# An attention and feed-forward kernel: first x block and v rows in order of use on one DMA queue, small loads behind them, and another order of the weight folds

## The chip, the cores and the metric

One core of one Trainium2 chip runs one program. The metric is the time of that program on the device, in microseconds, and lower is better. TensorE is called PE here, VectorE DVE, ScalarE ACT, GpSimd POOL and SyncE SP, as in the profile.

## The reference, cut to what matters

```python
# B=1, S=2048, D=640, H=32 heads of Dh=20, F=1728; bf16
g = sigmoid((x * gate_w).sum(-1, keepdims=True))
q, k, v = heads(x @ wqkv)                       # [H, S, Dh] each
phi(u)  = concat([softmax(u @ w_phi[h]), softmax(-(u @ w_phi[h]))])
kv, z   = phi(k).T @ v, phi(k).sum(over S)      # linear attention, not causal
a       = (phi(q) @ kv) / (phi(q) @ z + 1e-6) @ wo
b       = (gelu(x @ w_gate) * (x @ w_up)) @ w_down
out     = g * a + (1 - g) * b
```

`q @ w_phi` is linear in x, so the kernel multiplies `w_phi` into the key and query weights first. It calls this a fold: five folds for the keys and five for the queries, one for each 128 rows of the weights. The gate weights become one more column of the keys' weights.

## The kernel before

Only the first 30 us matter here. The x of the first four tiles of 128 tokens is loaded as it lies and transposed on PE. The x of the later tiles and the weights to be folded come by transposing DMA loads (`dma_start_transpose`, called turned loads below). All loads of the SP queue are issued in the order of the program. `sc.op` and `sc.dma` add the semaphore waits that the named reads and writes call for, so each engine's order is the order of the program.

```python
        x4 = self.x[0:self.BT, :].rearrange("(p j) n -> p j n", j=self.TB)

        def xload(q, j):                  # two rows of each group of four: 320 KB
            sc.dma(q, lambda e: e.dma_start(self.xtok[:, j:j + 2, :], x4[:, j:j + 2, :]), ...)
# ... (wload: one turned load of 640 x 640 weights; xturn(t, n): turned x of tiles t to t+n-1)
        sc.op("pool", lambda e: e.memset(self.gz[:, :], 0.0), writes=["gz"])
        xload("sp", 0)
        xload("act", 2)
        sc.dma("act", lambda e: e.dma_start(
            self.wphi_sb[:, :, :], self.wphi.rearrange("h d f -> (h d) f").rearrange("(i p) f -> p i f", p=P)),
            writes=["wphi"])
        for kt in range(KD):
            sc.dma("sp", lambda e: e.dma_start(self.w3[:, kt, 0:D], w3[:, kt, 2 * D:3 * D]), writes=[("wv", kt)])
        sc.dma("act", lambda e: e.dma_start(self.gz[0:KD, :], self.gw.rearrange("(k p) -> k p", p=P)), writes=["gz"])
        xturn(4, 2)
        wload(self.wkT, D, "wkT")
        xturn(6, 2)
        wload(self.wqT, 0, "wqT")
        xturn(8, 4)
        xturn(12, 4)
# ... (then the feed-forward weights)
```

The start of PE's program, and the order of the folds (`f`), of v (`v_early`), of the keys (`k_early`) and of the query projections (`pq`):

```python
        warm(7)                           # 7 matmuls of 512 columns on a zeroed tile
        xt(0, 6, "d"); xt(1, 7, "a"); xt(2, 2, "d"); xt(3, 3, "a")   # PE transposes, DVE or ACT copies
        # ... v of tiles 0-3, step by step over the five v rows: 4 x 2 matmuls for each row
        # ... before the last row: self.blockdiag() (w_phi), self.gate_column(6) (gate row, a PE transpose)
        self.v_early(4, 6)
        self.v_early(5, 0)
        f(0, "k", (2, 3), "d")
        f(1, "k", (4, 5), "a")
        self.v_early(6, 6)
        f(2, "k", (2, 3), "d")
        f(3, "k", (4, 5), "a")
        f(4, "k", (0, 1), "d")
        self.v_early(7, 6)
        self.k_early(0, 2)
        f(0, "q", (4, 5), "d")
        f(1, "q", (6, 7), "d")
        self.k_early(1, 0)
        f(2, "q", (4, 5), "d")
        f(3, "q", (6, 7), "d")
        self.k_early(2, 2)
        f(4, "q", (4, 5), "d")
        self.k_norm(0)
        self.k_early(3, 0)
        self.k_norm(1)
        self.pq(0, 1, 1)
        self.pq(0, 0, 0)
        self.pq(0, 3, 3)
        self.columns = True
        self.gram(0)
```

PE writes its results into numbered banks, and `pq` takes bank 6 or 7 in turn, so the third one waits until ACT has read the first one's bank:

```python
    def pq(self, b, i, n):
        sc = self.sc
        bank = 6 + n % 2
        # ... five matmuls, then two ACT exponentials out of that bank
```

`gram(t)` (PE's product of phi(k) and v for tile t) needs `k_norm(t)`: a sum, a reciprocal and two products on DVE, 1.48 + 0.55 + 1.56 us by the timeline.

The softmax here doesn't subtract the row's maximum and nothing guards it: scores larger than these inputs give would overflow.

Of the kernel before, what the change touches and what calls it, by code (L numbers as in the profile page):

```python
# [3 lines left out]
P = 128  # L4
BF16 = mybir.dt.bfloat16
F32 = mybir.dt.float32
AF = mybir.ActivationFunctionType
# [100 lines left out]
class _Kernel:  # L108
    S, D, H, DH, F = 2048, 640, 32, 20, 1728
    KD = D // P  # L110
# [31 lines left out]
    def alloc(self):  # L142
        nc = self.nc
        S, D, KD, NT, BT, NFC, DH = self.S, self.D, self.KD, self.NT, self.BT, self.NFC, self.DH
        T = nc.alloc_sbuf_tensor
        self.xT = T("xT", [P, KD, S], BF16)
        self.wo_sb = T("wo_sb", [P, KD, D], BF16)
        self.wg_sb = T("wg_sb", [P, KD, 13 * P], BF16)
        self.wu_sb = T("wu_sb", [P, KD, 13 * P], BF16)
        self.wgu_sb = T("wgu_sb", [P, KD, P], BF16)  # L150
        self.wd_sb = T("wd_sb", [P, NFC, D], BF16)
        self.Eq = T("Eq", [P, 2, KD, S], BF16)
        self.KV = T("KV", [P, KD, 2, self.HB * self.DB], BF16)
        self.hmask = T("hmask", [P, 2, KD, self.HB], BF16)
        self.mask = T("mask", [P, KD, 8], BF16)
        self.ident = T("ident", [P, P], BF16)
        self.zero = T("zero", [P, 512], BF16)
        self.gz = T("gz", [P, P], BF16)
        self.gcol = T("gcol", [P, NT], F32)
        self.gtmp = T("gtmp", [P, NT], F32)  # L160
        self.Gm = T("Gm", [P, NT], F32)
        self.Gr = T("Gr", [P, NT], F32)
        self.BD = T("BD", [P, KD, 8 * DH], BF16)
        self.wphi_sb = T("wphi_sb", [P, KD, DH], BF16)

        def place(lists):
            size = {"b": 0}
            plans = []
            for items in lists:
                c = 0  # L170
                for name, shape, dt in items:
                    n = mybir.dt.size(dt)
                    for s_ in shape[1:]:
                        n *= s_
                    c = (c + 31) // 32 * 32
                    plans.append((name, shape, dt, c))
                    c += n
                size["b"] = max(size["b"], c)
            arena = T("arena%d" % len(self._arenas), [P, size["b"]], mybir.dt.uint8)
            self._arenas.append(arena)  # L180
            base = nc.lookup_mloc(arena).addr
            for name, shape, dt, c in plans:
                setattr(self, name, nc.alloc_sbuf_tensor_at(name, shape, dt, offset=base + c))
        self._arenas = []
        place([
            [("w3", [P, KD, 2 * D + 2], BF16), ("wq2", [P, KD, D], BF16)],
            [("hT0", [P, NFC, BT], BF16), ("gl", [P, 3, BT], BF16)],
        ])
        place([
            [("Ek", [P, self.NSE, 2, D], BF16), ("vaug", [P, self.NSV, self.H, self.DA], BF16),  # L190
             ("Dk", [P, self.NSE, 2, 2 * self.H], F32)],
            [("hT1", [P, NFC, BT], BF16)],
        ])
        place([
            [("xtok", [P, self.TB, D], BF16), ("wkT", [P, KD, D], BF16), ("wqT", [P, KD, D], BF16)],
            [("goT", [P, 8, KD, P], BF16), ("O1", [P, 2, D], BF16), ("O2", [P, 2, D], BF16),
             ("Og", [P, 2, D], BF16), ("RH", [P, 2, 8, 2, 16], F32), ("outsb", [P, 4, D], BF16)],
        ])
        self.ps = nc.alloc_psum_tensor("ps", [P, 4096], F32)
# [8 lines left out]
    def loads(self):  # L208
        sc, nc = self.sc, self.nc
        D, KD, DH, P_ = self.D, self.KD, self.DH, P  # L210
        w3 = self.wqkv.rearrange("(kt p) n -> p kt n", p=P)

        x4 = self.x[0:self.BT, :].rearrange("(p j) n -> p j n", j=self.TB)

        def xload(q, j):
            sc.dma(q, lambda e: e.dma_start(self.xtok[:, j:j + 2, :], x4[:, j:j + 2, :]),
                   writes=[("xtok", j), ("xtok", j + 1)])

        def wload(T, c0, key):
            sc.dma("sp", lambda e: e.dma_start_transpose(T[:, :, :], self.wqkv[:, c0:c0 + D]), writes=[key])  # L220

        def xturn(t, n):
            a, z = t * P, (t + n) * P
            sc.dma("sp", lambda e: e.dma_start_transpose(self.xT[:, :, a:z], self.x[a:z, :]),
                   writes=[("xT", k) for k in range(t, t + n)])
        sc.op("pool", lambda e: e.memset(self.gz[:, :], 0.0), writes=["gz"])
        xload("sp", 0)
        xload("act", 2)
        sc.dma("act", lambda e: e.dma_start(
            self.wphi_sb[:, :, :], self.wphi.rearrange("h d f -> (h d) f").rearrange("(i p) f -> p i f", p=P)),  # L230
            writes=["wphi"])
        for kt in range(KD):
            sc.dma("sp", lambda e: e.dma_start(self.w3[:, kt, 0:D], w3[:, kt, 2 * D:3 * D]), writes=[("wv", kt)])
        sc.dma("act", lambda e: e.dma_start(self.gz[0:KD, :], self.gw.rearrange("(k p) -> k p", p=P)), writes=["gz"])
        xturn(4, 2)
        wload(self.wkT, D, "wkT")
        xturn(6, 2)
        wload(self.wqT, 0, "wqT")
        xturn(8, 4)
        xturn(12, 4)  # L240
        half = 7 * P
# [10 lines left out]
        for r in (0, 1):  # L252
            sc.dma("sp", lambda e: e.dma_start(self.wd_sb[64 * r:64 * r + 64, 13, :], self.wd[13 * P:self.F, :]),
                   writes=[("wd13", r)])
        sc.dma("sp", lambda e: e.dma_start(self.wo_sb[:, :, :], self.wo.rearrange("(kt p) n -> p kt n", p=P)),
               writes=["wo"])
# [61 lines left out]
    def fold(self, kt, which, banks, ekey):  # L318
        sc = self.sc
        DH = self.DH  # L320
        wT = self.wkT if which == "k" else self.wqT
        for i in range(self.KD):
            lo, hi = self.HLO[i], self.HHI[i]
            for h in (0, 1):
                a, z = max(lo, 16 * h), min(hi, 16 * h + 15)
                if a > z:
                    continue
                n = (z - a + 1) * DH
                b, c0, k0 = banks[h], (a - 16 * h) * DH, (a - lo) * DH
                first, fin = (i == 0 or a == 16), (z in (15, 31) and i in (2, 4))  # L330
                sc.op("pe", lambda e: e.matmul(  # L331
                    self.bank(b)[:, c0:c0 + n], wT[:, i, kt * P:(kt + 1) * P], self.BD[:, i, k0:k0 + n],
                    start=first, stop=fin, skip_group_check=True),
                    reads=["w%sT" % which, ("BD", i)], writes=[("ps", b)], signal=fin)
        src = self.pair(banks)
        if which == "k":
            dst = self.w3[:, kt, self.D:2 * self.D].rearrange("p (b c) -> p b c", c=320)
        else:
            dst = self.wq2[:, kt, :].rearrange("p (i r c) -> p r i c", r=2, c=64)
            src = src.rearrange("p r (i c) -> p r i c", c=64)  # L340
        rd = [("ps", b) for b in banks]
        wr = [("w%s2" % which, kt)]
        if ekey == "d":
            self.sc.op("dve", lambda e: e.tensor_copy(dst, src), reads=rd, writes=wr)
        else:
            self.sc.op("act", lambda e: e.activation(dst, src, AF.Copy), reads=rd, writes=wr)
# [161 lines left out]
                      writes=[("KV", i, r, g)])  # L508
                self.kvk[i, r].append(("KV", i, r, g))

    def pq(self, b, i, n):
        sc = self.sc
        bank = 6 + n % 2
        for kt in range(self.KD):
            self.mm(bank, 0, 512, self.wq2[:, kt, i * P:(i + 1) * P], self.xT[:, kt, b * self.BT:(b + 1) * self.BT],
                    kt == 0, kt == self.KD - 1, [("xT", t) for t in range(4 * b, 4 * b + 4)] + [("wq2", kt)])
# [15 lines left out]
    def attention_state(self):  # L532
        NT = self.NT
        order = [(b, i) for b in range(self.NB) for i in range(self.KD)]
        sc = self.sc
        sc.op("dve", lambda e: e.memset(self.zero[:, :], 0.0), writes=["zero"])

        def warm(n):
            for i in range(n):
                sc.op("pe", lambda e: e.matmul(self.bank(0), self.zero[:, 0:P], self.zero[:, :], start=True, stop=True),  # L540
                      reads=["zero"], writes=[("ps", 0)])
        vs, ve, xt = self.v_step, self.v_first_evac, self.x_transpose
        warm(7)
        xt(0, 6, "d")
        xt(1, 7, "a")
        xt(2, 2, "d")
        xt(3, 3, "a")
        for t in range(4):
            vs(t, 0)
        for t in range(4):  # L550
# [11 lines left out]
                ve([0, 1, 2], "a", True)  # L562
        ve([3], "d", True)
        f = self.fold
        self.v_early(4, 6)
        self.v_early(5, 0)
        f(0, "k", (2, 3), "d")
        f(1, "k", (4, 5), "a")
        self.v_early(6, 6)
        f(2, "k", (2, 3), "d")  # L570
        f(3, "k", (4, 5), "a")
        f(4, "k", (0, 1), "d")
        self.v_early(7, 6)
        self.k_early(0, 2)
        f(0, "q", (4, 5), "d")
        f(1, "q", (6, 7), "d")
        self.k_early(1, 0)
        f(2, "q", (4, 5), "d")
        f(3, "q", (6, 7), "d")
        self.k_early(2, 2)  # L580
        f(4, "q", (4, 5), "d")
        self.k_norm(0)
        self.k_early(3, 0)
        self.k_norm(1)
        self.pq(0, 1, 1)
        self.pq(0, 0, 0)
        self.pq(0, 3, 3)
        self.columns = True
        self.gram(0)
        self.k_norm(2)  # L590
# [2 lines left out]
        n = 4  # L593
# [47 lines left out]
    def num(self, t):  # L641
        sc = self.sc
        NBK = self.NUMB
        DB, DH = self.DB, self.DH
        old = [("xtok", k) for k in range(4)] + ["wkT", "wqT"]
        w = self.HB * DB
        for i in range(self.KD):
            for s in (0, 1):
# [190 lines left out]
```

## Time and profile before

| | before |
|---|---|
| time, median (range) of the 6 runs beside the changed kernel | 288.97 us (288.30 to 289.33) |
| span of the profiled run | 287.9 us |
| PE busy | 282.0 us, 98% |
| first x transposed / first v matmul / v of tile 4 | 4.72 / 6.40 / 12.29 us |
| key folds / query folds / first gram begin | 14.79 / 20.75 / 30.26 us |

The head of the page and the busy time of each engine:

```profile
span 287.9 us, 7001 instructions
...
PE 282.0 (98%) x3017; PEld 185.7 (65%) x3032; DVE 174.8 (61%) x353; ACT 105.0 (36%) x199; POOL 5.3 (2%) x36
...
```

PE has almost no idle time to give back. What is left lies in the first 30 us. The timeline of PE shows it; its columns are start, length, engine, line, operation, output<-inputs, form, count, and in brackets the idle time before and what ended it:

```profile
...
1.25 3.17 PE L540 MATMUL ps<-zero 128*128 128x512 bf16 x7 [1.25 <-DVE zero L536]
4.72 1.83 PE L290 MATMUL ps<-ident,xtok 128*128 128x128 bf16 x20 [0.30 <-DMA xtok<-in_A_x_dram]
6.40 4.69 PE L363 MATMUL ps<-w,xT 128*128 128x480 bf16 x32
...
12.29 2.67 PE L351 MATMUL ps<-w,xT 128*128 128x512 bf16 x19
14.79 0.79 PE L331 MATMUL ps<-BD,wkT 128*128 128x140 bf16 x12
15.45 1.53 PE L351 MATMUL ps<-w,xT 128*128 128x512 bf16 x10
...
20.75 0.80 PE L331 MATMUL ps<-BD,wqT 128*128 128x140 bf16 x12
...
26.63 2.10 PE L351 MATMUL ps<-xT,wq 128*128 128x512 bf16 x9
29.08 1.25 PE L351 MATMUL ps<-xT,wq 128*128 128x512 bf16 x5 [0.34 <-ACT Eq L518]
30.26 0.48 PE L449 MATMUL ps<-Ek,vaug 128*64 128x120 bf16 x11
...
```

The first 4.7 us are warm-up and waiting for x. From there PE runs through to 29.08, where the third query projection waits for ACT. The x19 at 12.29 is one matmul record short (20 were issued), so v of tile 4 really began about 0.2 us earlier. The warm-up matmuls start 0.427 us apart and the first transposes 0.107 us apart; from 5.90 us on the transposes are 0.056 us apart. The Trainium skill (TensorE: Matmul & The Clock Gate, Part 1) gives 106.7 and 426.7 ns for a cold array at 128 and 512 columns and about 56 ns for a warm one at 128, so this trace agrees. The page's row of granted clock shows 9 in every slice and does not tell the two apart.

The waits of PE and of its weight loads (PEld) in the first 32 us: engine, line, what it waited for, total us, times, longest.

```profile
...
PEld ps L290 <- DMA xtok<-in_A_x_dram: 1.2, 1, 1.2
...
PE ps L351 <- ACT Eq L518: 0.3, 1, 0.3
...
PEld ps L331 <- DMA wqT<-in_A_wqkv_dram: 0.3, 1, 0.3
...
```

The loads, by the list of DMA issues (queue, operation, count, KB each, median us from issue to landing):

```profile
...
w<-in_A_wqkv_dram SPq DMA_DIRECT2D x5, 160.0 KB, 4.0
...
xtok<-in_A_x_dram ACTq DMA_DIRECT2D x1, 320.0 KB, 3.6
xtok<-in_A_x_dram SPq DMA_DIRECT2D x1, 320.0 KB, 3.9
...
xT<-in_A_x_dram SPq DMA_TRANSPOSE x4, 5.4
...
wkT<-in_A_wqkv_dram SPq DMA_TRANSPOSE x1, 6.9
wqT<-in_A_wqkv_dram SPq DMA_TRANSPOSE x1, 8.8
...
```

In the trace each of these loads signals 16 times (the gate row 6 times), and the last signal is the landing. The two x pieces land at 4.43 and 4.68 us, the v rows from 5.26 to 7.23, the keys' weights at 13.11, the turned x of tiles 6 and 7 at 15.40, the queries' weights at 20.70. The last two are used at 15.45 and 20.75. So PE follows close behind the turned loads.

### The profile page before, as it was taken

To read this page: it belongs to the slowest core of one execution; us is meant where nothing else is said; L and a number is where in the kernel's file an instruction comes from. 1 tells how busy PE (TensorE), PEld (TensorE's weight loads), DVE (VectorE), ACT (ScalarE), POOL (GpSimd) and SP (SyncE) were. 2 spreads that over 40 slices of the span, in tenths; PEclk is the share of its full clock that TensorE was granted. 3 is DMA by queue.
4 is the path that set the end of the run, shared out by engine and by line. 5 is a ranking of instruction groups with operands and counts; after the bars stand their busy time and mean duration, and the time that the engine had idled before them with its cause. 6 is when DMAs were issued, how large, how long until landed. Compare 5 with 4: busy or idle time off the path is not lost.

```text
span 287.9 us, 7001 instructions
## 1 busy us (share of the span) xinstructions
PE 282.0 (98%) x3017; PEld 185.7 (65%) x3032; DVE 174.8 (61%) x353; ACT 105.0 (36%) x199; POOL 5.3 (2%) x36
## 2 busy tenths in 40 slices
PE   7999999999999999999999999999999999999996
PEld 4566689999994444444577544457754445777785
DVE  2338999999977553568588142258823324883801
ACT  3357897687663322322111332211133231112111
POOL 7000000000000000000000000000000000000000
PEclk9999999999999999999999999999999999999999
DMA  7999996000002000011014200001330000132221
GB/s 232 191 166 240 368 367 204 0 2 2 2 0 48 0 0 0 3 24 23 2 25 86 78 0 0 0 3 25 57 96 11 0 0 2 25 45 78 67 72 48
DMA packets 36937, 18.67 MB, mean 65 GB/s; under 512 B 28970, under 2 KB 36394, under 8 KB 36906
## 3 DMA queue, kind: packets, MB, share of 16 engines
q1 hardware_dynamic: 36096, 17.86, 24.8%
q8 instruction: 24, 0.39, 0.6%
q10 hardware_dynamic: 810, 0.35, 0.5%
q14 instruction: 7, 0.06, 0.1%
HBM read 9.04 MB, written 2.62 MB: 40 GB/s over the span
## 4 chain that ended last, share of the span: by engine, by line
PE 96%; DMA 1%; ACT 1%; issue 1%; ACTq 0%
PE ps L351 60%; PE ps L708 28%; PE ps L651 2%; PE ps L363 2%; PE ps L449 2%; DMA xtok<-in_A_x_dram 1%; PE ps L331 1%; PE ps L290 1%; ACT Ek L413 0%; ACT Eq L518 0%; ACT outsb L721 0%; ACT gcol L416 0%; PE ps L313 0%; ACTq L42 0%
## 5 line engine op out<-in xcount | busy, mean ns | idle before, releaser
L625 DVE TENSOR_TENSOR hT<-ps,gl 128x512 bf16<-128x512 f32 x52 | 35.7, 690 | 65.1 <-PE ps L351 65.0
L708 PE MATMUL ps<-wd_sb,hT 64*128 64x320 bf16 (+2 forms) x918 | 66.2, 288 | 0.0
L351 PE MATMUL ps<-xT,wg_sb 128*128 128x512 bf16 (+1 forms) x265 | 63.8, 379 | 0.6 <-issue 0.5
L351 PE MATMUL ps<-xT,wu_sb 128*128 128x512 bf16 (+1 forms) x263 | 63.3, 379 | 0.5 <-issue 0.2
L623 ACT ACTIVATE gl<-ps 128x512 bf16<-128x512 f32 x52 | 30.9, 596 | 70.3 <-PE ps L351 66.0
L708 PEld LDWEIGHTS ps<-wd_sb,hT 64*128 64x128 bf16 x918 | 43.1, 94 | 15.6 <-ACT gl L623 0.8
L351 PEld LDWEIGHTS ps<-xT,wu_sb 128*128 128x128 bf16 (+1 forms) x270 | 26.5, 99 | 29.7 <-DVE hT L625 0.5
L351 PEld LDWEIGHTS ps<-xT,wg_sb 128*128 128x128 bf16 (+1 forms) x270 | 26.0, 99 | 29.1 <-issue 0.5
L721 ACT ACTIVATE outsb<-ps,Gm 128x320 bf16<-128x320 f32 (+2 forms) x31 | 14.5, 515 | 75.6 <-PE ps L708 75.6
L351 PE MATMUL ps<-w,xT 128*64 128x512 bf16 (+6 forms) x398 | 41.6, 325 | 0.2
L351 PEld LDWEIGHTS ps<-w,xT 128*64 128x64 bf16 (+1 forms) x400 | 35.8, 107 | 4.8
L708 PE MATMUL ps<-wo_sb,goT 64*128 64x320 bf16 (+2 forms) x340 | 27.8, 288 | 0.0
L351 PE MATMUL ps<-xT,wq 128*64 128x512 bf16 (+1 forms) x184 | 26.1, 380 | 0.4 <-ACT Eq L518 0.3
L433 DVE TENSOR_TENSOR Ek<-Ek,Dk 128x640 bf16<-128x640 bf16 x32 | 25.0, 822 | 0.6
L678 DVE TENSOR_TENSOR O<-ps,RH 128x640 bf16<-128x640 f32 x32 | 24.7, 814 | 0.0
L424 DVE TENSOR_REDUCE Dk<-Ek 128x64 f32<-128x1280 bf16 x16 | 23.7, 1479 | 0.1
L413 ACT ACTIVATE Ek<-ps 128x640 bf16<-128x640 f32 x32 | 20.7, 703 | 3.7 <-PE ps L351 3.7
L518 ACT ACTIVATE Eq<-ps 128x512 bf16<-128x512 f32 x40 | 21.7, 605 | 1.1 <-PE ps L351 0.8
L708 PEld LDWEIGHTS ps<-wo_sb,goT 64*128 64x128 bf16 x340 | 16.1, 94 | 5.4
L351 PEld LDWEIGHTS ps<-xT,wq 128*64 128x64 bf16 (+1 forms) x185 | 15.3, 108 | 3.4 <-ACT Eq L518 0.8
L405 ACT ACTIVATE vaug<-ps 128x640 bf16<-128x640 f32 x12 | 8.5, 706 | 12.1 <-PE ps L351 12.1
L667 DVE RECIPROCAL RH<-ps 128x32 f32<-128x32 f32 x16 | 5.7, 357 | 7.5 <-PE ps L651 6.8
(65 smaller groups left out, 148.0 us busy)
## 6 DMA issues: line engine op xcount, KB each, us to landing
out_dram<-outsb SPq DMA_DIRECT2D x7, 320.0 KB, 2.3
wd_sb<-in_B_w_down_dram SPq DMA_DIRECT2D x1, 2080.0 KB, 14.2
wg_sb<-in_B_w_gate_dram SPq DMA_DIRECT2D x1, 1120.0 KB, 5.8
wu_sb<-in_B_w_up_dram SPq DMA_DIRECT2D x1, 1120.0 KB, 8.3
wg_sb<-in_B_w_gate_dram SPq DMA_DIRECT2D x1, 960.0 KB, 9.6
wu_sb<-in_B_w_up_dram SPq DMA_DIRECT2D x1, 960.0 KB, 10.2
w<-in_A_wqkv_dram SPq DMA_DIRECT2D x5, 160.0 KB, 4.0
wo_sb<-in_A_wo_dram SPq DMA_DIRECT2D x1, 800.0 KB, 9.9
```

The costliest lines, as they stand in the source:

```text
L351: self.sc.op("pe", lambda e: e.matmul(self.ps[a:z, bank * 512 + c0:bank * 512 + c0 + n], lhs[:, a:z], rhs, start=first, stop=fin), reads=r ...
L363: sc.op("pe", lambda e, c0=c0, n=n, bk=bk, col=col: e.matmul(self.bank(bk)[:, col:col + n], self.xT[:, kt, t * P:(t + 1) * P], self.w3[:, ...
L405: self.sc.op("act", lambda e: e.activation(self.vaug[:, sv, :, 0:self.DH], self.bank(B, self.D).rearrange("p (h d) -> p h d", d=self.DH), ...
L413: self.sc.op("act", lambda e, s=s, scale=scale: e.activation(self.Ek[:, se, s, :], self.ps[:, o:o + self.D], AF.Exp, scale=scale), reads=[ ...
L424: sc.op("dve", lambda e: e.tensor_reduce(self.Dk[:, se, 0, :].rearrange("p (s h) -> p s h", h=H), self.Ek[:, se, :, :].rearrange("p s (h d ...
L433: sc.op("dve", lambda e, v=v, r=r: e.tensor_tensor(v, v, r, ALU.mult), reads=[("Rk", se)], writes=[("Ek", se, s)])
L518: sc.op("act", lambda e, s=s, scale=scale: e.activation(self.Eq[:, s, i, b * self.BT:(b + 1) * self.BT], self.bank(bank), AF.Exp, scale=sc ...
L623: sc.op("act", lambda e: e.activation(self.gl[:, slot, :], self.bank(banks[0]), AF.Gelu_apprx_tanh), reads=[("ps", banks[0])], writes=[("g ...
L625: sc.op("dve", lambda e: e.tensor_tensor(hT[:, c, :], self.bank(banks[1]), self.gl[:, slot, :], ALU.mult), reads=[("ps", banks[1]), ("gl", ...
L678: dve(lambda e, o=o, f=f, s=s: e.tensor_tensor(o, V[s][:, :, :, 0:DH], f, ALU.mult), rb + [key(6 + s)], [("O", s, sl)], guard=old)
L708: sc.op("pe", lambda e: e.matmul(self.bank(bk, w), lhs, rhs, start=opens and x == 0, stop=end and not opens, skip_group_check=True), reads ...
L721: sc.op("act", lambda e: e.activation(dst, self.bank(bk, w), AF.Copy, scale=g), reads=rd, writes=wr)
```

## The change

Its intent is that each transfer comes in the order of its use. The x block comes in four pieces and v in one row and two pairs, all on the SP queue; the two small loads go out later on the ACT queue, behind an ACT copy. The warm-up reads a constant, so that it starts sooner. The key folds stand in a row, the query folds behind the second keys, so that neither waits for its weights. The third query projection gets bank 0.

```diff
         def xload(q, j):
-            ...(self.xtok[:, j:j + 2, :], x4[:, j:j + 2, :])
+            ...(self.xtok[:, j, :], x4[:, j, :])
 # ... (a helper vload; wload split by rows, used for all rows at once)
-        xload("sp", 0)
-        xload("act", 2)
-        sc.dma("act", ... wphi ...)
-        for kt in range(KD):
-            sc.dma("sp", ... v row kt ...)
-        sc.dma("act", ... gate row ...)
+        sc.op("act", ... activation(gtmp, const 1.0, AF.Exp))     # loads ACT's table early
+        for j in range(self.TB):
+            xload("sp", j)
+        for a, z in ((0, 1), (1, 3), (3, 5)):
+            vload("sp", a, z)
         xturn(4, 2)
 # ...
-        warm(7)
+        for n in (512, 512, 512, 512, 512, 512, 128, 128):
+            ... matmul(self.bank(0, n), ones[:, 0:P], ones[:, 0:n])   # a constant, no memset
         xt(0, 6, "d")
         xt(1, 7, "a")
         xt(2, 2, "d")
-        xt(3, 3, "a")
+        xt(3, 3, "d")
+        sc.dma("act", ... wphi ...)
+        sc.dma("act", ... gate row ...)
 # ...
-        v 4, v 5, k fold 0, 1, v 6, k fold 2, 3, 4, v 7, keys 0, q fold 0, 1, keys 1,
-        q fold 2, 3, keys 2, q fold 4, k_norm(0), keys 3, k_norm(1), pq 1, pq 0, pq 3
+        v 4, v 5, k fold 0, 1, 2, 3, 4, v 6, keys 0, v 7, keys 1, q fold 0, 1, keys 2,
+        q fold 2, 3, keys 3 (first half), q fold 4, keys 3 (second half), k_norm(0), k_norm(1),
+        pq 1, pq 0, pq 3 in bank 0
```

The last hunk is told in words; PSUM banks change with it.

More of the change, by code (lines that the diff above doesn't have):

```diff
@@ L156, in alloc @@
         self.ident = T("ident", [P, P], BF16)
-        self.zero = T("zero", [P, 512], BF16)
         self.gz = T("gz", [P, P], BF16)
@@ L215, in xload, with vload, wload @@
         def xload(q, j):
-            sc.dma(q, lambda e: e.dma_start(self.xtok[:, j:j + 2, :], x4[:, j:j + 2, :]),
-                   writes=[("xtok", j), ("xtok", j + 1)])
-        def wload(T, c0, key):
-            sc.dma("sp", lambda e: e.dma_start_transpose(T[:, :, :], self.wqkv[:, c0:c0 + D]), writes=[key])
+            sc.dma(q, lambda e: e.dma_start(self.xtok[:, j, :], x4[:, j, :]), writes=[("xtok", j)])
+        def vload(q, a, z):
+            sc.dma(q, lambda e: e.dma_start(self.w3[:, a:z, 0:D], w3[:, a:z, 2 * D:3 * D]),
+                   writes=[("wv", kt) for kt in range(a, z)])
+        def wload(T, c0, key, a, z):
+            sc.dma("sp", lambda e: e.dma_start_transpose(T[:, :, a * P:z * P], self.wqkv[a * P:z * P, c0:c0 + D]),
+                   writes=[(key, k) for k in range(a, z)])
         def xturn(t, n):
@@ L226, in loads @@
         sc.op("pool", lambda e: e.memset(self.gz[:, :], 0.0), writes=["gz"])
-        xload("sp", 0)
-        xload("act", 2)
-        sc.dma("act", lambda e: e.dma_start(
-            self.wphi_sb[:, :, :], self.wphi.rearrange("h d f -> (h d) f").rearrange("(i p) f -> p i f", p=P)),
-            writes=["wphi"])
-        for kt in range(KD):
-            sc.dma("sp", lambda e: e.dma_start(self.w3[:, kt, 0:D], w3[:, kt, 2 * D:3 * D]), writes=[("wv", kt)])
-        sc.dma("act", lambda e: e.dma_start(self.gz[0:KD, :], self.gw.rearrange("(k p) -> k p", p=P)), writes=["gz"])
+        sc.op("act", lambda e: e.activation(self.gtmp[:, 0:1], self.nc.const_aps.tensor(1.0, [P, 1], BF16), AF.Exp),
+              writes=["gtmp"])
+        for j in range(self.TB):
+            xload("sp", j)
+        for a, z in ((0, 1), (1, 3), (3, 5)):
+            vload("sp", a, z)
         xturn(4, 2)
-        wload(self.wkT, D, "wkT")
+        wload(self.wkT, D, "wkT", 0, 5)
         xturn(6, 2)
-        wload(self.wqT, 0, "wqT")
+        wload(self.wqT, 0, "wqT", 0, 5)
         xturn(8, 4)
@@ L333, in fold @@
                     start=first, stop=fin, skip_group_check=True),
-                    reads=["w%sT" % which, ("BD", i)], writes=[("ps", b)], signal=fin)
+                    reads=[("w%sT" % which, kt), ("BD", i)], writes=[("ps", b)], signal=fin)
         src = self.pair(banks)
@@ L509, in kv_mask, with pq @@
                 self.kvk[i, r].append(("KV", i, r, g))
-    def pq(self, b, i, n):
+    def pq(self, b, i, n, bank=None):
         sc = self.sc
-        bank = 6 + n % 2
+        bank = 6 + n % 2 if bank is None else bank
         for kt in range(self.KD):
@@ L535, in attention_state @@
         sc = self.sc
-        sc.op("dve", lambda e: e.memset(self.zero[:, :], 0.0), writes=["zero"])
-        def warm(n):
-            for i in range(n):
-                sc.op("pe", lambda e: e.matmul(self.bank(0), self.zero[:, 0:P], self.zero[:, :], start=True, stop=True),
-                      reads=["zero"], writes=[("ps", 0)])
+        ones = self.nc.const_aps.tensor(1.0, [P, 512], BF16)
+        for n in (512, 512, 512, 512, 512, 512, 128, 128):
+            sc.op("pe", lambda e: e.matmul(self.bank(0, n), ones[:, 0:P], ones[:, 0:n], start=True, stop=True),
+                  writes=[("ps", 0)])
         vs, ve, xt = self.v_step, self.v_first_evac, self.x_transpose
-        warm(7)
         xt(0, 6, "d")
@@ L546, in attention_state @@
         xt(2, 2, "d")
-        xt(3, 3, "a")
+        xt(3, 3, "d")
+        sc.dma("act", lambda e: e.dma_start(
+            self.wphi_sb[:, :, :], self.wphi.rearrange("h d f -> (h d) f").rearrange("(i p) f -> p i f", p=P)),
+            writes=["wphi"])
+        sc.dma("act", lambda e: e.dma_start(self.gz[0:self.KD, :], self.gw.rearrange("(k p) -> k p", p=P)), writes=["gz"])
         for t in range(4):
@@ L564, in attention_state @@
         f = self.fold
-        self.v_early(4, 6)
-        self.v_early(5, 0)
+        ve, ke = self.v_early, self.k_early
+        ve(4, 6)
+        ve(5, 0)
         f(0, "k", (2, 3), "d")
         f(1, "k", (4, 5), "a")
-        self.v_early(6, 6)
-        f(2, "k", (2, 3), "d")
-        f(3, "k", (4, 5), "a")
-        f(4, "k", (0, 1), "d")
-        self.v_early(7, 6)
-        self.k_early(0, 2)
+        f(2, "k", (6, 7), "d")
+        f(3, "k", (0, 1), "a")
+        f(4, "k", (2, 3), "d")
+        ve(6, 4)
+        ke(0, 6)
+        ve(7, 0)
+        ke(1, 2)
         f(0, "q", (4, 5), "d")
         f(1, "q", (6, 7), "d")
-        self.k_early(1, 0)
+        ke(2, 0)
         f(2, "q", (4, 5), "d")
         f(3, "q", (6, 7), "d")
-        self.k_early(2, 2)
+        self.proj(3, 640, 384, 2, 128, ["wk2"])
         f(4, "q", (4, 5), "d")
+        self.proj(3, 1024, 257, 3, 0, ["wk2", "wgate"])
+        self.k_evac(3, 2)
         self.k_norm(0)
-        self.k_early(3, 0)
         self.k_norm(1)
@@ L586, in attention_state @@
         self.pq(0, 0, 0)
-        self.pq(0, 3, 3)
+        self.pq(0, 3, 3, 0)
         self.columns = True
@@ L644, in num @@
         DB, DH = self.DB, self.DH
-        old = [("xtok", k) for k in range(4)] + ["wkT", "wqT"]
+        old = [("xtok", k) for k in range(4)] + [(w, k) for w in ("wkT", "wqT") for k in range(self.KD)]
         w = self.HB * DB
```

## The prediction

> **What bounds it now.** TensorE. The busy table gives PE 282.0 of 287.9 us (98%), and the chain of waits is 96% PE. From 4.72 us on PE is nearly gapless. In the order of time (instruction timeline, chain):
> - 0.80 to 4.68 us: the load of the first x block (two 320 KB transfers, one per queue, 3.6 and 3.9 us to landing). PE runs 7 warm-up matmuls, begun at 1.25 us after a DVE memset, 0.427 us apart.
> - 4.72 to 6.40: 20 transposes, the first 0.107 us apart, from about 5.9 us on 0.056.
> - 6.40 to 12.29: v of tiles 0-3, about 0.3 us of it waiting for xT copies.
> - 26.6 to 30.3: a hole of about 0.4 us where the third q projection waits for the ACT exponentials of the bank it shares.
> Fold weights are near their limit too: keys' weights land at 13.1 us (used 14.8), the turned x of tiles 6-7 at about 15.5 (used 15.58), the queries' weights at 20.66 (used 20.75, waits view 0.3 us).
>
> **What the change does.**
> 1. x arrives in four 160 KB pieces on one queue in front of v. Estimate from the before trace (first packets 1 to 1.4 us after issue, about 350 GB/s, signal 0.6 us after the last packet): the first piece lands at 3.0-3.3 us, the fourth at 4.3-4.7, first v row at 4.7-5.2. The Trainium skill (DMA: Bandwidth & Descriptors, "Issuing engines are not separate DMA queues") says that queues share the same engines; the gain is order, not bandwidth.
> 2. Warm-up reads a constant, no DVE wait: starts at about 0.9 and ends at about 3.7 us. The early transposes still run at half speed: the skill (TensorE: Matmul & The Clock Gate, Part 1) has 107 against 56 ns and a free-running window; this trace shows the same two spacings. So 20 transposes end at 5.2-5.8 us. First v matmul at about 5.5 instead of 6.40; v ends at about 11.2 instead of 12.29.
> 3. wphi and the gate row go out behind an ACT copy (about 5.5 us), land at about 8-9.5. The gate transpose comes at about 9.8: small risk.
> 4. k folds in a row (1.6 us of PE, evacuations 0.82 DVE, 0.70 ACT over three bank pairs): start about 13.8, the keys' weights just landed. v of tile 6 then meets xT 6-7 at about 15.5: wait 0-0.3 us. The q folds move behind the second keys (+1.37 us): about 21.0, past the queries' weights.
> 5. Third q projection into bank 0: the Eq wait goes. But the first key normalisation (1.48+0.55+1.56 = 3.6 us DVE) still follows the last q evacuation: about 25.8 to 29.4. PE reaches the first gram at about 28.7 and waits about 0.7 us. It starts at 29.4 instead of 30.3.
> Then the order is unchanged: PE needs 3.8-4.1 us a tile, DVE 3.58; the shift is kept.
>
> **Total.** About 1.1 us won at the front, some 0.2 given back at landings and the first gram: 0.9 us. Predicted 288.1 us, range 287.2 to 288.9. Faster by over 2%: 1%; within 2%: 98%; slower: 1%.
>
> **Right if:** first transpose at about 3.7 us, first v matmul at 5.2-5.8, q folds at about 21, a new PE wait on DVE Ek before the first gram, first gate/up matmul about 0.9 us earlier.
>
> **Wrong if:** the clock rises earlier or later against the work (±0.4 us); the gate row or wphi lands late beside the transposing loads and stalls PE at about 10 us; the turned loads land later because seven issues precede them (each 0.1 us late counts in full at the folds).

## The result, and the profile after

The changed kernel took 289.74 us (median of 6, 289.20 to 290.48) against 288.97 before. The ratio is 1.0032, with a 95% interval of 1.0013 to 1.0051. Ratios here are the mean time of one kernel's runs over that of the other's of the same rounds, so not quite the ratio of the medians. It is slower, by about 0.9 us in the means; 288.1 was predicted. The two profiled runs themselves took 289.17 us (before) and 289.71 us (after), so the pages differ by less than the means do.

The head of the page:

```profile
span 288.5 us, 7003 instructions
...
PE 282.2 (98%) x3018; PEld 186.1 (65%) x3033; DVE 174.7 (61%) x353; ACT 104.5 (36%) x199; POOL 5.3 (2%) x36
...
```

The timeline of PE:

```profile
...
0.84 2.93 PE L539 MATMUL ps<-const-bfloat16-1.0 128*128 128x512 bf16 x8 [0.84 <-PEq L829]
3.56 1.81 PE L291 MATMUL ps<-ident,xtok 128*128 128x128 bf16 x15
5.63 0.72 PE L291 MATMUL ps<-ident,xtok 128*128 128x128 bf16 x5 [0.26 <-DMA xtok<-in_A_x_dram]
6.14 1.36 PE L364 MATMUL ps<-w,xT 128*128 128x480 bf16 x8
7.93 3.45 PE L364 MATMUL ps<-w,xT 128*128 128x480 bf16 x24 [0.43 <-DMA w<-in_A_wqkv_dram]
...
12.58 2.67 PE L352 MATMUL ps<-w,xT 128*128 128x512 bf16 x19
15.09 1.96 PE L332 MATMUL ps<-BD,wkT 128*128 128x140 bf16 x30
17.09 5.39 PE L352 MATMUL ps<-w,xT 128*128 128x512 bf16 x39
22.32 0.79 PE L332 MATMUL ps<-BD,wqT 128*128 128x140 bf16 x12
...
30.88 0.32 PE L450 MATMUL ps<-Ek,vaug 128*64 128x120 bf16 x5 [0.82 <-DVE Ek L434]
```

Its waits:

```profile
...
PEld ps L450 <- DVE Ek L434: 1.3, 1, 1.3
...
PE ps L450 <- DVE Ek L434: 0.8, 1, 0.8
...
PEld ps L364 <- DMA w<-in_A_wqkv_dram: 0.8, 1, 0.8
PEld ps L291 <- DMA xtok<-in_A_x_dram: 0.5, 1, 0.5
PE ps L364 <- DMA w<-in_A_wqkv_dram: 0.4, 1, 0.4
...
PE ps L291 <- DMA xtok<-in_A_x_dram: 0.3, 1, 0.3
...
```

Its loads:

```profile
...
xtok<-in_A_x_dram SPq DMA_DIRECT2D x4, 160.0 KB, 2.6
w<-in_A_wqkv_dram SPq DMA_DIRECT2D x2, 320.0 KB, 5.0
...
w<-in_A_wqkv_dram SPq DMA_DIRECT2D x1, 160.0 KB, 3.3
...
wphi_sb<-in_A_w_phi_dram ACTq DMA_DIRECT2D x1, 25.0 KB, 5.9
...
wkT<-in_A_wqkv_dram SPq DMA_TRANSPOSE x1, 7.6
wqT<-in_A_wqkv_dram SPq DMA_TRANSPOSE x1, 7.4
...
```

PE begins its transposes at 3.56 us, 1.16 us earlier, as planned. The first v matmul is only 0.26 us earlier (6.14 against 6.40), because the fourth x piece is late. Then v waits for its second row until 7.93, and v of tile 4 begins 0.29 us *later* (12.58 against 12.29). From there on to the first gram 0.33 us more is lost (30.88 against 30.26 in all): PE stands 0.82 us before the first gram, waiting for DVE.

| landing (last signal), us | before | after | estimated in the prediction |
|---|---|---|---|
| first x piece | 4.43 (two tiles) | 3.03 | 3.0-3.3 |
| last x piece | 4.68 | 5.59 | 4.3-4.7 |
| first v row | 5.26 | 6.00 | 4.7-5.2 |
| second v row | 5.87 | 7.89 | |
| last v row | 7.23 | 8.80 | |
| keys' weights | 13.11 | 14.00 | 13.1 |
| turned x of tiles 6-7 | 15.40 | 16.70 | 15.5 |
| gate row | 5.66 | 10.74 | 8-9.5 |

### The profile page after: what moved, and what is told of

It reads as the page before. It is cut to its first block, busy times and chain, and to the rows that moved or that the text cites. A ratio compares the mean times of both kernels' runs of the same rounds, so it can differ in the third digit from the quotient of the medians.

```text
span 288.5 us, 7003 instructions
## 1 busy us (share of the span) xinstructions
PE 282.2 (98%) x3018; PEld 186.1 (65%) x3033; DVE 174.7 (61%) x353; ACT 104.5 (36%) x199; POOL 5.3 (2%) x36
## 4 chain that ended last, share of the span: by engine, by line
PE 94%; DMA 2%; DVE 1%; issue 1%; SPq 1%; ACT 0%; DVEq 0%
PE ps L352 59%; PE ps L713 28%; PE ps L656 2%; PE ps L450 2%; DMA w<-in_A_wqkv_dram 2%; PE ps L364 2%; PE ps L332 1%; SPq L215 1%; DVE Dk L425 1%; DVE wq L345 0%; DVE Ek L434 0%; DVE Dk L429 0%; SPq L218 0%; ACT outsb L726 0%; PE ps L314 0%
```

## The experiments

The time goes with the start of the first feed-forward work: across the profiled runs of the experiments, the time less the start of the first gate matmul (of the feed-forward, after the attention state) is 209.2 to 209.9 us. So the differences arise before it, up to these 0.7 us. One profile is one run, and runs of one kernel differ by over 1 us. Profiles say where the time was spent in one of them.

| run | what it is | median us | ratio to before | 95% interval |
|---|---|---|---|---|
| again | the changed kernel again | 289.86 | 1.0042 | 1.0024-1.0061 |
| front | loads and warm-up of the change, old folds | 290.48 | 1.0057 | 1.0041-1.0073 |
| folds | old loads, fold order and bank 0 of the change | 289.04 | 1.0008 | 0.9993-1.0022 |
| x_two_queues | changed, x as two pieces on two queues | 291.13 | 1.0078 | 1.0065-1.0092 |
| gz_early | changed, small loads early | 289.85 | 1.0040 | 1.0021-1.0060 |
| gz_early_x2 | changed, small loads early, x on two queues | 289.07 | 1.0024 | 1.0004-1.0043 |
| gz_early_vrows | changed, small loads early, five v rows | 289.56 | 1.0028 | 1.0011-1.0045 |
| gz_first | changed, gate row ahead of w_phi | 290.04 | 1.0050 | 1.0033-1.0067 |
| x_only | before, x in four pieces on one queue | 290.31 | 1.0045 | 1.0026-1.0064 |
| v_only | before, v as 1+2+2 rows | 289.31 | 1.0005 | 0.9984-1.0027 |
| warm_only | before, constant warm-up | 289.62 | 1.0017 | 0.9986-1.0048 |
| bank0 | before, third pq in bank 0 | 288.28 | 0.9974 | 0.9954-0.9994 |
| x4_two_queues | before, x in four pieces on two queues | 288.72 | 1.0000 | 0.9980-1.0019 |
| x2_one_queue | before, x in two pieces on one queue | 289.14 | 1.0015 | 0.9998-1.0033 |
| candidate | before, x4_two_queues + warm_only + bank0 | 288.97 | 1.0005 | 0.9985-1.0026 |
| folds_pq2 | folds, fourth pq ahead of the first gram | 288.52 | 0.9994 | 0.9978-1.0011 |
| cand_old_warm | candidate with the old warm-up | 288.88 | 1.0000 | 0.9984-1.0016 |
| warm_long | before, constant warm-up of 8 x 512 | 288.55 | 0.9989 | 0.9972-1.0005 |

The medians of before in the five groups (of four, four, four, three and three runs) were 288.85, 288.63, 289.14, 288.94 and 288.94 us.

### First group: which half

**again** has no edit.

> The changed kernel once more, for a second profile. In its first profile the four x pieces landed at 3.03, 3.57, 4.60 and 5.59 us and the v transfers at 6.00, 7.89 and 8.80 us (medians over their 16 engines' signals: 2.93, 3.45, 3.99, 4.74, 5.14, 7.06, 8.75), and first gram began at 30.9 us. Theory A (the one-queue order of small pieces is slow by itself): the second profile shows the third v row landing again after 7 us and a wait of PE for v of at least 0.3 us; time 0.2 to 0.5% above before. Rival theory B (a chance disturbance of that one profile): v rows 1-2 land before 6.5 us, no PE wait for v, and the time is at most 0.1% above before.

Measured +0.42%. The second v row landed at 7.98 us and PE waited 0.7 us for it, then 0.5 us for the gate row (landed 11.91). Theory A passed and chance (B) is out.

**front** puts the old fold order and the old `pq` back into the changed kernel.

```diff
-        f(0..4, "k") in a row; q folds behind keys 1; pq(0, 3, 3, 0)
+        the order before; pq(0, 3, 3)
```

> Only the first part of the change: new load order, warm-up on the constant, wphi and gate row behind an ACT copy; folds and the third q projection as before. Theory A (the loss is in the loads): v ends at about 12.6 us as in the changed kernel (12.29 before), later than before by 0.2-0.5 us, and the time is 0.1 to 0.2% above before. Rival C (the loss is in the fold order): time at or below before, down to -0.3%.

Measured +0.57%: the loss is in the loads, and it looks larger with the old folds than with the new, though the intervals overlap. In its profile the key folds, right after v of tiles 4 and 5, began at 14.96 us against 14.79 before, so v was only 0.17 us late in that run, which was the fastest of the six; it waited for the fourth x piece (landed 6.09) and later for the turned x of tiles 6-7 (15.99). The expected size was too small.

**folds** is the reverse.

```diff
 # loads and warm-up as before
+        f(0..4, "k") in a row; q folds behind keys 1; pq(0, 3, 3, 0)
```

> Only the second part: five k folds in a row, q folds behind the second keys, third q projection in bank 0; loads as before. Theory A': v ends at 12.3 us as before, q folds start 9.8 us after (22.1), the first gram 8.45 us after that (30.55, with about 0.8 us of PE waiting for the first key normalisation): +0.1 to +0.3 us against before, +0.03 to +0.1%. Rival C (all the loss is here): +0.8 us, +0.3%. If the fold order gained what it was meant for: -0.3 us or better.

Measured +0.08%, not clear of zero, as theory A' said. Query folds began at 22.05 us and the first gram at 30.61. Its waits show the price of the order:

```profile
...
PEld ps L449 <- DVE Ek L433: 1.3, 1, 1.3
...
PE ps L449 <- DVE Ek L433: 0.8, 1, 0.8
...
```

**x_two_queues** takes the x loads of before into the changed kernel.

```diff
-        for j in range(self.TB):
-            xload("sp", j)                # one row each
+        xload("sp", 0)                    # two rows each
+        xload("act", 2)
```

> The changed kernel with the x block again in two pieces of 320 KB, one on each queue, all else as changed. Theory A (one queue with 160 KB pieces and 1280-byte packets is what is slow): x lands at 4.4-4.7 us, v rows in turn at 5.3 to 7.2 us as before, no PE wait for v; v ends at about 12.3; time between before and the changed kernel, about 0.1% above before. Theory D (the grouped v transfers are slow, two rows in each): v rows 1-2 land again after 7 us and PE waits for them; the time is at or above the changed kernel's.

The loads behaved as A said: v landed at 4.91, 6.81 and 7.74 us and PE did not wait for it. But the time rose to +0.78%, which neither theory had. The PE timeline shows why:

```profile
...
12.70 0.23 PE L315 MATMUL ps<-ident,gz 128*128 128x128 bf16 x1 [2.23 <-DMA gz<-in_gate_w_dram]
...
```

The transpose of the gate row stood 2.23 us, because the gate row, issued at 5.87 us on the ACT queue, landed at 12.65. This was named as a small risk in the prediction.

### Second group: the gate row

**gz_early** moves the two small loads back to the start.

```diff
+        sc.dma("act", ... wphi ...)      # before the ACT table load
+        sc.dma("act", ... gate row ...)
 # ...
         xt(3, 3, "d")
-        sc.dma("act", ... wphi ...)
-        sc.dma("act", ... gate row ...)
```

> The changed kernel with the two small transfers (w_phi and the gate row) issued on the ACT queue at the start, as before the change, instead of behind the first ACT copy; nothing else. Theory G (most of the loss is the gate row, which lands anywhere from 10.3 to 12.7 us when it is issued at 5.4 behind the turning loads, while its transpose on PE is due at 10 to 11): it lands by about 6 us, PE does not wait before the gate transpose, and the time falls to +0.0 to +0.2% of before, with less spread between runs. Rival theory A (most of the loss is x and v on one queue): the wait for the second v row (0.6 to 0.9 us in two profiles) stays and the time stays at +0.3 to +0.5%.

The gate row landed at 3.83 us and PE did not wait for it; the time stayed at +0.40%. Theory G fell for the changed kernel: there v is itself so late that the gate row mostly lands in time.

**gz_early_x2** has both edits: x in two pieces on two queues, and the small loads early, behind the second x piece on the ACT queue.

> As gz_early, and the x block again in two pieces of two rows on the two queues. In the earlier run with two queues and the late gate row, v began at 5.8 us and its fourth row at 9.2 (before: 6.4 and 9.8), then PE waited 2.2 us for the gate row. Theory G: without that wait v ends at about 11.7 us, 0.6 before the old kernel; the fold order gives back about 0.2 to 0.3: -0.1 to -0.2% of before. Rival A': if v now waits for its rows, no better than before.

Against x_two_queues the small loads' place is worth 2.25 - 0.53 = 1.7 us (differences of means to before in each group). So the late gate row does cost, once the x loads no longer hide it. But the version is still at +0.24%, not below before as expected. Its profile, with v of tile 4 at 11.27 us, fell on its fastest run (288.63 of 288.63 to 289.97). In that run the rest went as the prediction had it: no wait at the turned x of tiles 6-7 (landed 13.87, used 15.78), query folds at 21.00 us (predicted 21.0) and the first gram at 29.56 (29.4), with the wait before it below. It does not say what held the slower runs back.

```profile
...
PE ps L455 <- DVE Ek L439: 0.8, 1, 0.8
...
```

**gz_early_vrows** has gz_early's edit and this:

```diff
-        for a, z in ((0, 1), (1, 3), (3, 5)):
+        for a, z in ((0, 1), (1, 2), (2, 3), (3, 4), (4, 5)):
```

> As gz_early (x in four pieces on one queue), with v in five single rows as before instead of one row and two pairs. If the pairs are what lands v late (theory D): row 2 lands by 6.6 us, no PE wait for v, v ends at about 11.8 and time -0.1% of before. If the x pieces ahead of it are (theory A): row 2 lands at 6.5 to 7.2 us, PE still waits up to 0.5 us somewhere in v, v ends at about 12.1, time within 0.1% of before.

The second v row landed at 6.72 us and v waited for none, but the fourth x piece landed at 5.83. The turned x of tiles 6-7 landed at 16.94, and v of tile 6 waited 0.7 us for it. +0.28%: more than expected; the x pieces, not the v pairs.

**gz_first** swaps the two small loads.

```diff
-        sc.dma("act", ... wphi ...)
         sc.dma("act", ... gate row ...)
+        sc.dma("act", ... wphi ...)
```

> The changed kernel with the gate row issued ahead of w_phi in the same late place on the ACT queue. Theory G1 (it is late because the 640 pieces of 40 bytes of w_phi stand ahead of it): it lands 2 us or more earlier, by about 9 us, and PE never waits for it; time near gz_early's. Theory G2 (anything issued on the ACT queue at that time waits behind the turning loads already queued): it lands at 10 us or later all the same and the time stays at +0.3% or above.

The gate row landed at 9.28 us instead of 10.74 and 11.91 and PE did not wait for it. It was also issued 0.85 us earlier (4.50 against 5.35), so the rest, 0.6 to 1.8 us, may come from `w_phi` no longer ahead of it. The time, +0.50%, is near gz_early's as G1 said and above +0.3% as G2 said, so it does not decide.

### Third group: one edit at a time on the kernel before

**x_only**

```diff
-        xload("sp", 0)
-        xload("act", 2)
+        for j in range(self.TB):
+            xload("sp", j)                # one row each
```

> The kernel before with one edit: the x block in four 160 KB pieces on the SP queue ahead of v, w_phi and gate row early on the ACT queue as before. Theory A (the x pieces on one queue are the loss): the fourth piece lands at 5.2 to 6.1 us as in the changed kernel (second of two: 4.7 before), the keys' weights about 0.5 to 1 us later than 13.1, and the time rises by 0.2 to 0.4%. Rival (pieces are harmless and what lost was their company): fourth piece by 4.8 us, within 0.1% of before, or faster.

+0.45%: this edit alone loses as much as the whole change. The fourth piece landed at 5.78 us, the keys' weights at 14.01, the turned x of tiles 6-7 at 16.79, and v of tile 6 waited for it. The waits:

```profile
...
PEld ps L350 <- DMA xT<-in_A_x_dram: 1.6, 1, 1.6
PE ps L350 <- DMA xT<-in_A_x_dram: 1.4, 1, 1.4
...
```

**v_only**

```diff
-        for kt in range(KD):
+        for a, z in ((0, 1), (1, 3), (3, 5)):
 # ... (the load itself takes rows a to z-1)
```

> The kernel before with one edit: v in one row and two pairs instead of five rows. Theory D (pairs land late or slow the turning loads): second v row lands at 6.8 us or later (5.87 before), PE waits for it, +0.1 to +0.3%. Theory A: no wait longer than 0.2 us, within 0.1% of before.

The second row did land at 6.81 us, as D said, but PE did not wait for it, because each v row is four tiles' work (1.09 us). +0.05%: no loss found.

**warm_only**

```diff
-        warm(7)                           # zeroed tile
+        for n in (512, 512, 512, 512, 512, 512, 128, 128): ...   # constant
```

> The kernel before with one edit: the warm-up on the constant (begins at 0.84 us instead of 1.25, ends at about 3.6 instead of 4.2). Theory W (an earlier and shorter warm-up leaves a hole of 1.1 us before x lands and the clock rises later or drops again): +0.1 to +0.3%. Rival: [...]the transposes run faster on average, -0.1 to 0.0%.

+0.17% with an interval from -0.14 to +0.48%: inconclusive. Its runs went from 288.23 to 290.60 us.

**bank0**

```diff
-        self.pq(0, 3, 3)
+        self.pq(0, 3, 3, 0)
```

> The kernel before with one edit: the third q projection in bank 0. It takes away the wait for the ACT exponentials (0.35 to 0.5 us in the profile before) and the first key normalisation is done at 29.7 us, before PE would need it at 29.9: first gram 0.3 to 0.4 us earlier, -0.1 to -0.14%. Rival: the normalisation becomes the wait and nothing is gained.

-0.26%, clear of zero (-0.46 to -0.06%), and the expected size is inside the interval. First gram at 29.84 us instead of 30.26; PE no longer waits for ACT there:

```profile
...
29.84 0.46 PE L449 MATMUL ps<-Ek,vaug 128*64 128x120 bf16 x11
...
```

This is the one part of the change for which a gain was measured, and alone it beats both kernels (its interval lies below 1, and the changed kernel's, 1.0013 to 1.0051 in other rounds, above). It rests on six runs that were not repeated, and it is one of 18 intervals.

### Fourth group: queue or size, and a better version

**x4_two_queues** (against x_only)

```diff
-        for j in range(self.TB):
-            xload("sp", j)
+        xload("sp", 0)
+        xload("act", 1)
+        xload("sp", 2)
+        xload("act", 3)
```

> The kernel before with one edit: the x block in the same four 160 KB pieces as the change, but pieces 0 and 2 on the SP queue and 1 and 3 on the ACT queue. Theory Q (one queue alone is what delivers slowly while x and v start up): as many bytes have landed at 4.5 us as before (about 750 KB against 460 to 650 with all of it on one queue), v complete by 7.0 us, keys' weights and x of tiles 6-7 by 13 and 15.4 us, time within 0.1% of before or faster. Theory S (small pieces with 1280-byte packets are slow on any queue): 460 to 650 KB at 4.5 us, x of tiles 6-7 after 16 us, +0.3% or more.

0.00% (interval -0.20 to +0.19%): on two queues the same small pieces cost nothing that these runs show. The turned x of tiles 6-7 landed at 15.40 us, as before.

**x2_one_queue**

```diff
         xload("sp", 0)
-        xload("act", 2)
+        xload("sp", 2)
```

> The kernel before with one edit: the x block in its two 320 KB pieces, both on the SP queue. Theory Q: slow all the same, 500 to 650 KB at 4.5 us, x of tiles 6-7 at 16 us or later, +0.3 to +0.5%. Theory S: 750 KB at 4.5 us as before, within 0.1% of before.

+0.15%, interval -0.02 to +0.33%: between the theories. By bytes it was as fast as before (735 KB of x and v at 4.5 us, 1300 KB at 6.0), so one queue alone is not slow either. In its profile v began 0.77 us earlier than before (5.63), and PE then waited for the turned x of tiles 6-7, which landed at 15.77:

```profile
...
PE ps L351 <- DMA xT<-in_A_x_dram: 1.0, 1, 1.0
...
```

The table gives the KB of x and v (of 1440) whose packets had ended, from the trace's packet records:

| x block | kernels profiled | KB at 4.5 us | KB at 6.0 us | last v packet ends, us |
|---|---|---|---|---|
| two queues, either size | 12 (with before) | 703-805 | 1150-1288 | 6.67-7.45 |
| one queue, two pieces | 1 | 735 | 1300 | 6.74 |
| one queue, four pieces | 7 (with after and again) | 457-655 | 931-1021 | 7.85-9.37 |

The groups do not overlap at 4.5 or 6.0 us. In these runs it takes both, small pieces and one queue. The small pieces also have smaller packets (1280 bytes, against 2560 in the 320 KB pieces), and no run separates the two.

The issue rate alone does not explain it: SP issued x_only's pieces 0.47 us apart and had issued all four (640 KB) by 2.6 us, yet at 4.0 us only 366 KB had ended (633 before). A rival remains for part of x_only's loss: its three more issues on SP also push back what follows, so its first turned load was issued at 5.05 us, against 4.22 in x4_two_queues and 3.74 before. The profiles say that this is not all. Where that load was issued at 4.09 to 4.22 us, the turned x of tiles 6-7 landed at 15.33 to 15.77 in the four kernels without four pieces on one queue (x4_two_queues, x2_one_queue, candidate, cand_old_warm) and at 15.99 to 17.94 in the five with them (after, again, front, gz_early, gz_first).

A 1280-byte packet took 66 ns on average in x_only and 57 in before (there v rows only). Of all x and v packets, 19 to 28 took over 0.3 us in the seven kernels with four pieces on one queue, the longest 1.3 us (in after), and 5 to 19 in the others. Why is open.

**candidate** joins x4_two_queues, warm_only and bank0.

> A version meant to beat both: the kernel before, with the x block in four pieces on two queues, the constant warm-up, and the third q projection in bank 0. If theory Q holds, the first gram begins 0.3 us earlier for the bank (measured -0.26%) and up to 0.7 us for the earlier x: -0.3 to -0.5%. If S holds, +0.1% or worse.

+0.05%: it did not beat before. The hoped-for gain did not come.

### Fifth group: the rest

**folds_pq2**

```diff
         self.columns = True
+        self.pq(0, 2, 2)
         self.gram(0)
         self.k_norm(2)
-        self.pq(0, 2, 2)
```

> The kernel folds (old loads, new fold order) with the fourth q projection moved ahead of the first gram, so that PE has 1.08 us of work in the 0.8 us in which it waits for the first key normalisation. If that wait is what the fold order costs: PE no longer waits there, at most 0.4 us comes back as a wait at the second gram (the DVE chain has 3.58 us a tile), and the time goes from +0.08% to about -0.1%. If the cost of the order lies elsewhere: time unchanged at +0.08%.

-0.06%, near the expected -0.1%, but its interval overlaps that of folds. By the profiles the first gate matmul came at 79.45 us instead of 79.86, but 0.15 us of that was there already at the key folds (14.67 against 14.82). The wait of 0.8 us is gone; 0.2 us for ACT came in its place (and 0.2 us of waiting for DVE at the next gram):

```profile
...
PEld ps L351 <- ACT Eq L518: 0.7, 1, 0.7
...
PE ps L351 <- ACT Eq L518: 0.2, 1, 0.2
...
```

**cand_old_warm** puts `warm(7)` back into the candidate.

> The candidate with the old warm-up (seven matmuls on a zeroed tile) in place of the constant one. Theory W (the constant warm-up that stops at 3.6 us is worth -0.2 to +0.3 us at best and costs on average): -0.25% of before, as bank0 and the two-queue pieces add up to, with less spread than the candidate's. Rival: the same as the candidate, +0.05%.

0.00%, the same as the candidate: the warm-up is not what held it back. Its profile says what did. The key folds began at 13.85 us, 0.94 us earlier than before (14.79), and then PE waited (a line of the timeline, two of the waits):

```profile
...
13.85 0.79 PE L332 MATMUL ps<-BD,wkT 128*128 128x140 bf16 x12
...
PEld ps L352 <- DMA xT<-in_A_x_dram: 1.2, 1, 1.2
PE ps L352 <- DMA xT<-in_A_x_dram: 1.0, 1, 1.0
...
```

PE reached v of tile 6 and waited 1.0 us for the turned x, which landed at 15.64 us. The first gram began at 29.87, no earlier than bank0's 29.84.

**warm_long**

```diff
-        for n in (512, 512, 512, 512, 512, 512, 128, 128):
+        for n in (512,) * 8:
```

> The kernel before with the warm-up on the constant, but eight full matmuls (0.84 to about 4.25 us), so that it ends as late as the old one does. If the early end, with its hole of 1.1 us before x, is what made the constant warm-up slow or uneven (289.54 mean, 288.2 to 290.6): mean within 0.1% of before and spread as before (0.45 us). If the constant itself or the earlier start is: +0.15% and a wide spread again.

-0.11%, interval -0.28 to +0.05%, spread 0.30 us (standard deviation) against 0.94 in warm_only. It fits the idea that the early end of the warm-up makes runs uneven, but cand_old_warm speaks against it, and no interval is clear of the other. This stays open.

## Why the prediction was wrong

It said 288.1 us, range 287.2 to 288.9; 289.74 was measured.

- **Wrong, the step that failed: point 1, "the fourth at 4.3-4.7, first v row at 4.7-5.2", worked out from "about 350 GB/s".** That rate was read where two queues were loading together and carried over to four small pieces on one. They landed at 5.59 and 6.00 us, and the last v row at 8.80. Hence "v ends at about 11.2 us" was off by 1.4 us (12.58), which is nearly all of the 1.5 us by which the first gram missed (30.88 against 29.4). x_only shows that this edit alone costs 0.45%, and x4_two_queues that the same pieces on two queues cost nothing measurable. "The gain is order, not bandwidth", argued from the skill's page, was wrong here. The last risk under "Wrong if" came true with it: the first turned load was issued 0.4 us later (4.13 against 3.74), and the turned x of tiles 6-7 landed 1.3 us later.
- **Open: what an earlier front is worth.** Point 4 allowed 0-0.3 us of waiting for the turned x at about 15.5 us. With the old fold order more is lost there: cand_old_warm reached the key folds 0.94 us early and gave 1.0 us back at that load. With the new order v of tile 6 comes 1.35 us later after v of tile 4 (17.09 - 12.58 against 15.45 - 12.29), which can hide late turned loads: the profile of gz_early_x2, with v done early, met no wait there. That the loads cost 0.57% beside the old folds and the whole change only 0.32 and 0.42% points the same way, though the intervals overlap. But gz_early_x2 was still at +0.24% over its six runs, so the gain that the prediction counted on was not seen.
- **Right: the distances after v.** Query folds were put 9.8 us after the end of v and the first gram 8.4 us after those; measured 9.7 and 8.6. The wait before the first gram was put at 0.7 us and measured 0.82. The order was unchanged after it and the shift was kept.
- **Right: the fold order gives a little back.** The prediction's distances after v are 0.2 us longer than before (18.2 against 18.0 from v of tile 4 to the first gram); folds came to +0.08%, or 0.2 us, not clear of zero. Bank 0 alone was worth -0.26%, so by these means the new order gives that gain back. The profile shows the DVE wait in its place. folds_pq2 supports this with a profile, though not with separate intervals.
- **The gate row** landed later than the 8 to 9.5 us of point 3 (10.3 to 12.7 in the profiles of front, after, again and x_two_queues). The risk was named rightly but called small. PE stood 2.2 us for it where x came early (x_two_queues), and moving it early gained nothing clear in the changed kernel (gz_early).
- **The clock** switched at 3.9 to 6.4 us in the profiles that record it. No experiment gave it a cost, and how much of the spread of the runs it makes is not shown.

Open are why four small pieces on one queue deliver slowly, the warm-up's effect, and why gz_early_x2 is still at +0.24%.

## What to carry to other kernels

Before reordering loads for an early start, list every later landing that an engine meets with little slack: here PE met the turned x with 0.05 us to spare in the profile before, so with the old fold order an early front arrived early at the next wait (1.0 us in cand_old_warm), and a delay of that load was paid for (in x_only it landed 1.39 us later and PE waited 1.44 us). Do not carry a transfer rate from two queues with large pieces to one queue with small ones; measure the landings. And when a wait on one engine is removed, look for the next producer due at the same place, as the DVE normalisation was here.

## What the Trainium skill lacked or had wrong

- DMA: Bandwidth & Descriptors, "Issuing engines are not separate DMA queues": it says that issuing from several engines saves only the issue time. Here the same four 160 KB pieces put on two queues instead of one moved 1197 KB instead of 967 KB of x and v by 6.0 us and changed the time from +0.45% to 0.00%. Issue time may be part of it (the first v row was issued at 1.75 us instead of 2.67) but not all: with the first turned load issued at the same 4.1 to 4.2 us, the turned x of tiles 6-7 landed by 15.77 us in every profile without four pieces on one queue and not before 15.99 with them.
- DMA: Bandwidth & Descriptors, "Rules for kernel authors": it says that below 64 KB a transfer is mostly overhead. This is no contradiction but a number for a case above that size: on one queue 160 KB pieces (packets of 1280 bytes) moved 967 KB by 6.0 us and 320 KB pieces (2560 bytes) 1300 KB.
- TensorE: Matmul & The Clock Gate, Part 1: its two spacings were met (0.107 and 0.056 us at 128 columns), and the switch came 2.85 to 5.6 us after the first matmul in the 17 profiles that record it. The page gives about 4 us ±0.5 of sustained matmuls, and says elsewhere that it varies with the free-running window; the range here is the wider one, but PE also stood for up to 0.95 us in that time (warm_only).
- No page that was read here gives a time for a small load on the ACT queue beside turned loads on the SP queue: a 1.2 KB row issued at 5.87 us behind `w_phi` (x_two_queues) landed 6.8 us later, against 3.9 us when issued early (at 1.72 us, before).
